# GpSimd sums that wait for the VectorE sum ahead of them in the list

## The chip, the cores and the metric

The kernel runs on one core of a Trainium2 chip. The metric is the device time of one execution in microseconds. The five engines of the core work in parallel, each through its own queue in order: TensorE (PE in the profile) multiplies matrices, VectorE (DVE) and ScalarE (ACT) do elementwise work and empty the matmul results, GpSimd (POOL) does elementwise work between tiles in SBUF and issues the loads, SyncE (SP) issues the stores. An engine waits for another by a semaphore.

## The reference

Eight batches of eight heads, 576 tokens, head dimension 64, 32 memory slots; then a bilinear feed-forward block over all 4608 tokens.

```python
def _attn_ref(q, k, v, phi):
    a = phi - np.max(phi, axis=2, keepdims=True)
    a = np.exp(a)
    a = a / (np.sum(a, axis=2, keepdims=True) + 1e-09)
    k_m = np.einsum('bhsm,bhsd->bhmd', a, k)
    v_m = np.einsum('bhsm,bhsd->bhmd', a, v)
    scores = scale * np.matmul(q, k_m.transpose(0, 1, 3, 2))
    ...
    attn = attn / (np.sum(attn, axis=-1, keepdims=True) + 1e-09)
    return np.matmul(attn, v_m)

def _moe_ref(x, w_a, w_b, w_out):      # x: 4608 x 512, w_a and w_b: 512 x 1536, w_out: 1536 x 512
    a = x @ w_a
    b = x @ w_b
    return a * b @ w_out
```

## The kernel before

**An order written out by hand.** The whole kernel is a list of some 1,500 short steps, the string `PLAN`. A loop at the end reads it from left to right and calls one function for each step; each function appends its instructions to the queues of its engines. So the list sets the order of the instructions on every engine, and two engines are tied to each other only by the data that they hand on. The steps of eight batches are interleaved, so that the attention of the later batches runs between the feed-forward matmuls of the earlier ones.

**The steps that matter here.** `a4.7.0` is one half of the product of attention and folded weights for batch 4, block 7 of 128 columns of the hidden layer, first half of the tokens: two matmuls into a PSUM bank `pa` (L724), copied by ScalarE to `a_sb` (L728). `b4.7.0` does the same for the other weight into `pb`, and VectorE multiplies `a_sb` by `pb` into `ht` (L731). One operand of that product lies in PSUM. `d3` takes three matmuls of the last matrix product (`two_downs`, L651), and now and then the sums that empty its banks. `6ed`, `6sm0`, `6tn0`, `6tn1`, `6ad` belong to the softmax over the slots of batch 6: a transposition, sums, normalisation on GpSimd and VectorE, a transposition back. `7exp0` is an exponential on ScalarE. `v7`, `p5`, `q3` and so on issue loads from GpSimd's queue.

**Seven products instead of eight.** From batch 5 on, many of the 2x2 block products of the hidden layer are done in seven matmul products instead of eight (function `seven`, steps such as `P5.4.6`), and so are the last ones (`two_downs`). This needs sums and differences of the operands beforehand, all of them between tiles in SBUF:

- `h8.2` and `g8.3`: sums of the hidden layer for the last product, 128x768 (`sum_tokens`, L635), four for each pair of blocks; `h` on GpSimd, `g` on VectorE.
- `5S11P`, `5S01D`: sums of the folded weights of batch 5, 128x512 (`v_sum`, L530); `P` on GpSimd, `D` on VectorE. The first digit behind S is which sum, the second which third of the columns. `P5.4.6` needs `5S11P`, `P5.4.5` needs `5S21P`.
- `5T1P`, `5T2D`: sums of the attention of batch 5, 128x288 (`a_sum`, L538), with the same letters.
- `T30` on GpSimd and `V31` on VectorE: sums of the last weights, 128x768 (`sum_weights`, L618).
- `H7.4` on GpSimd and `J5.4` on VectorE: the products that finish a block of `seven` (L778).

All of these, and the normalisations of L475 and L499, are `tensor_tensor` instructions with two operands in SBUF. Which engine takes a step is written in its name.

**PSUM.** Its eight banks are given out in turn by `Banks`; a tile that takes a bank waits until the last reader of the bank's former tile is done.

Of the kernel before, what the change touches and what calls it, by code (L numbers as in the profile page):

```python
# [11 lines left out]
ALU = mybir.AluOpType  # L12
# [32 lines left out]
a3.10.1 b3.10.1 a3.8.1 b3.11.0 a3.2.1 h5.3 d3 a3.5.1 d1 5tn0 b3.5.1 6qt0 d1 a3.7.1 a3.11.1 b3.7.1 d2 6exp0 4x0b1 d1  # L45
a4.0.0 b3.2.1 d4 a3.9.1 5sm1 h6.0 d1 b3.8.1 h6.1 d3 5tn1 d2 4v2b 4x2b0 4x2b1 4v1a 4x1a1 6kv 4v2a 4x2a0 d1 q7 6km1 d1
6km0 d3 a3.4.1 b3.4.1 4x1a0 d1 g6.2 b3.11.1 h7.3 d4 b3.9.1 6qt3 d4 a4.0.1 a4.2.1 d3 6kvt d5 h7.0 5ad 4x2a1 5T0P d4 6sc
6e0 5v1a d2 5x1a1 b4.0.1 b4.2.1 a4.3.0 d7 6e1 7qt0 5x1a0 a4.9.1 d1 b4.3.0 b4.0.0 a4.1.1 a4.6.0 7qt3 5v0a 5T2D 5x0a0
5v0b 5v1b 5x1b0 5x0a1 g7.1 g8.0 d1 5T1P 5T3P g7.2 5x1b1 b4.6.0 5S01D g8.1 d3 v7 5S11P 5S21P a4.7.0 5S31P d1 g8.3 d3
h8.2 d3 6ed d3 P5.4.1 d2 b4.7.0 d1 5x0b1 d3 a4.6.1 b4.6.1 5x0b0 5S00P d4 7exp0 6sm0 d3 a4.2.0 b4.2.0 d1 a4.9.0 P5.4.6  # L50
b4.1.1 a4.10.1 6tn0 d3 b4.9.0 P5.4.5 d1 P5.4.7 a4.1.0 b4.1.0 a4.8.0 b4.8.0 a4.4.1 d5 P5.4.2 P5.4.4 P5.5.1 P5.5.2
P5.4.3 d2 a4.4.0 b4.4.0 d2 7qt2 d2 P5.5.5 d2 b4.9.1 P5.5.6 a4.5.0 d3 P5.5.3 a4.11.0 b4.5.0 5v2a 5x2a0 5x2a1 5v2b
a4.10.0 6sm1 d1 5S10P b4.10.1 5x2b1 d1 5S30P 5x2b0 d2 P5.5.7 b4.4.1 a4.7.1 a4.3.1 5S20P d2 b4.10.0 d2 P5.5.4 b4.11.0
b4.7.1 J5.4 6tn1 P5.1.1 a4.11.1 a4.8.1 d3 P5.1.6 g9.0 h9.3 d1 P5.1.2 d2 h9.1 P5.2.1 H5.5 b4.8.1 P5.1.5 d5 P5.2.5 d1
P5.2.2 P5.1.7 a4.5.1 P5.2.6 P5.1.3 d4 P5.6.1 h9.2 d1 H5.1 P5.1.4 P5.2.3 P5.2.7 a5.11.0 P5.7.1 b4.3.1 H5.2 d4 P5.7.2
P5.6.5 P5.2.4 b4.11.1 d1 P5.7.6 b4.5.1 h10.0 d6 P5.6.6 P5.6.2 P5.7.5 P5.7.7 h10.3 P5.6.3 d2 P5.6.7 a5.10.1 P5.0.1 d4
b5.10.1 P5.7.4 7exp1 a5.8.0 P5.7.3 d3 H5.6 P5.0.5 d1 P5.6.4 6ad H5.7 P5.3.1 P5.0.6 6T0P d2 b5.8.0 d3 a5.8.1 P5.0.3
P5.0.2 P5.0.7 d5 P5.3.6 a5.10.0 d3 6T1P 6T3P P5.3.5 P5.0.4 P5.3.7 P5.3.2 d4 P5.3.3 H5.0 d3 P5.3.4 H5.3 6v0a 6x0a1 7kv
7km1 6x0a0 6v0b 6x0b0 6v2b 6x2b1 7km0 6T2P d2 6x2b0 d6 7qt1 d4 a5.11.1 b5.11.0 a5.9.0 b5.10.0 6x0b1 7kvt d1 b5.9.0 d5
h10.1 6v1a 6x1a0 7sc 7e0 6x1a1 d1 g10.2 6S00P 6S10D 6S20D d1 g11.0 d1 b5.11.1 7e1 d4 b5.8.1 d5 6v1b 6x1b0 6S01P 7v1a  # L60
g11.1 6v2a d1 6S30D 6x2a1 d5 a5.9.1 7x1a0 d3 7ed 7x1a1 d1 7sm0 d8 b5.9.1 6x1b1 P6.3.1 P6.1.1 d4 7sm1 6x2a0 P6.1.2
h11.2 P6.3.2 6S11P 6S31P d4 P6.3.5 d2 P6.3.6 d4 a6.11.0 P6.3.3 d1 P6.3.7 a6.10.1 b6.11.0 g11.3 d1 P6.1.5 H6.3 6S21D
a6.8.0 d2 P6.2.5 7tn1 d2 g12.0 a6.10.0 P6.2.1 P6.3.4 P6.1.6 d2 h12.1 d4 P6.2.2 P6.2.6 P6.2.3 P6.1.3 P6.1.7 d2 P6.0.1
d5 P6.0.5 d1 P6.2.7 d2 P6.6.1 H6.2 P6.0.6 d2 P6.1.4 d1 P6.2.4 H6.1 d4 h12.2 d1 P6.0.2 P6.6.6 d2 P6.0.7 b6.10.0 d2
P6.5.1 P6.6.5 d2 P6.0.4 P6.6.7 a6.9.0 P6.0.3 7tn0 H6.0 P6.5.6 d1 P6.6.2 d1 P6.6.3 H6.6 d5 P6.5.2 7ad 7T0P d1 P6.4.1
P6.5.5 P6.5.7 d3 P6.4.5 h12.3 P6.6.4 d6 P6.4.6 P6.4.2 P6.4.3 P6.5.4 P6.5.3 H6.5 d5 P6.7.5 d1 P6.4.7 P6.7.1 d5 7T1P
b6.8.0 P6.4.4 d2 P6.7.6 P6.7.3 7v0a 7x0a0 7v1b 7x1b1 P6.7.7 7x0a1 b6.9.0 d2 7x1b0 d2 P6.7.2 P6.7.4 d4 a6.8.1 d2 7T3D
7v2b 7x2b1 7S01D 7S11D 7v2a g13.0 7x2a1 J6.7 7x2a0 7v0b d1 a6.11.1 d4 g13.1 d10 7S21D d1 7x0b0 d2 7S31D g13.2 J6.4
7S00D h13.3 7x0b1 P7.4.1 7T2D d2 b6.10.1 d2 7x2b0 7S10P d2 P7.4.2 d5 P7.4.6 b6.11.1 d1 P7.4.5 P7.7.1 P7.7.2 a7.8.0 d2
P7.4.3 P7.5.1 a6.9.1 P7.4.7 P7.7.6 b6.8.1 b7.8.0 b6.9.1 7S30P H7.4 d1 P7.4.4 d1 P7.7.5 P7.7.7 d4 7S20P P7.5.2 a7.11.0  # L70
d1 a7.10.0 P7.5.6 d4 P7.7.3 P7.7.4 P7.6.1 b7.10.0 P7.5.5 a7.9.0 P7.5.7 J7.7 P7.6.6 d5 P7.1.1 d2 h14.0 g14.1 d1 P7.5.3
H7.5 P7.5.4 d2 P7.1.5 P7.6.2 h14.2 P7.6.5 P7.6.7 P7.1.6 d2 b7.11.0 d2 P7.0.1 P7.1.3 P7.1.7 P7.6.3 h14.3 P7.6.4 d6
P7.0.2 d8 H7.1 P7.1.2 b7.9.0 P7.2.1 P7.0.5 P7.0.6 P7.1.4 d4 P7.2.2 P7.3.1 d1 P7.2.5 P7.0.7 P7.0.3 d1 H7.0 d5 P7.2.6 d1
P7.0.4 H7.6 P7.3.6 d1 a7.10.1 P7.2.7 b7.10.1 P7.3.5 P7.3.7 a7.9.1 d3 P7.3.2 d3 P7.2.4 P7.3.4 a7.8.1 g15.0 g15.1 g15.2
# [6 lines left out]
def kernel(  # L81
# [11 lines left out]
    nc = tc.nc  # L93

    B, H, S, D = q.shape
# [6 lines left out]
    HALF = S // 2  # L102
# [70 lines left out]
    def load_w(x, lo, hi):  # L173
        nc.gpsimd.dma_start(out=w_sbs[x][:, :, lo:hi], in_=(wa_rows, wb_rows)[x][:, :, lo:hi])
# [6 lines left out]
    ht = consts.tile([P, NFF, 2 * S], F16, name="ht")  # L181
# [51 lines left out]
    nc.vector.memset(kv_sbs[0][:, 2], 1.0 / CS)  # L233
    for x in halves:
        nc.vector.tensor_copy(out=kvs[0][:, 0, x], in_=k_f32[:, x])
    def issue(x):

        b, _, half = x[1:].partition(".")
        if x[0] == "w":
            lo, hi = x[2:].split(":")  # L240
            load_w("ab".index(x[1]), int(lo), int(hi))
        elif x[0] == "o":
            load_wo(int(b))
        elif x[0] == "p":
# [19 lines left out]
    attn = {}  # L264
# [13 lines left out]
    def units(b):  # L278
# [4 lines left out]
        t = {}  # L283
# [181 lines left out]
        def normalise(g, hfs=slice(0, 2)):  # L465
            if b not in attn:
                attn[b] = mid.tile([P, 2, S], F16, name="A")
            sl = slice(tokens(b, hfs.start).start, tokens(b, hfs.stop - 1).stop)
            if ("R", 0) not in t:
                both = spare.tile([P, 3, 512], F16, name="vsum1").rearrange("p z n -> p (z n)")  # L470
                for x in range(2):
                    t["R", x] = both[:, S * x:S * (x + 1)]
            nc.scalar.activation(out=t["R", g][:, sl], in_=t["L", g][:, sl], func=AF.Exp, scale=-1.0)
            engine = nc.vector if b < 2 else nc.gpsimd
            engine.tensor_tensor(out=attn[b][:, g, sl], in0=t["E"][:, g, sl], in1=t["R", g][:, sl], op=ALU.mult)  # L475

        def pairs(x):
            return x.rearrange("p g s -> p (g s)").bitcast(F32)
# [43 lines left out]
        def v_sum(n, y, engine):  # L522
            if (b, n) not in vsums:
                vsums[b, n] = spare.tile([P, 3, 512], F16, name=f"vsum{n}")
            S1, S2, S4 = (vsums[b, n][:, z] for z in range(3))
            sl = slice(512 * n, 512 * (n + 1))
            (A11, A12), (S3, A22) = ([vabs[b][z][:, g, sl] for g in range(2)] for z in range(2))
            out, in0, in1, op = ((S3, A11, S3, ALU.subtract), (S2, A22, S3, ALU.subtract), (S1, S2, A11, ALU.add),
                                 (S4, A12, S2, ALU.subtract))[y]
            engine.tensor_tensor(out=out, in0=in0, in1=in1, op=op)  # L530

        def a_sum(y, engine):
            if b not in asums:
                asums[b] = mid.tile([P, 4, HALF], F16, name="asum")
            T1, T2, T3, T4 = (asums[b][:, z] for z in range(4))
            (B11, B12), (B21, B22) = ([attn[b][:, g, HALF * z:HALF * (z + 1)] for z in range(2)] for g in range(2))
            out, in0, in1 = ((T1, B12, B11), (T2, B22, T1), (T3, B22, B12), (T4, B21, T2))[y]
            engine.tensor_tensor(out=out, in0=in0, in1=in1, op=ALU.subtract)  # L538

        def take_fold(lo, hi, z, gs=range(2)):  # L540
            first, second = b == 0 and hi <= 512, b < 2
# [71 lines left out]
    def sum_weights(x, part, engine):  # L613
        t = [t1_sum] + [w_sums[:, y] for y in range(3)]
        out, in0, in1 = ((t[0], quarter(0, 1), quarter(0, 0)), (t[1], quarter(1, 1), t[0]),
                         (t[2], quarter(1, 1), quarter(0, 1)), (t[3], quarter(1, 0), t[1]))[x]
        sl = slice(KH // 2 * part, KH // 2 * (part + 1))
        engine.tensor_tensor(out=out[:, sl], in0=in0[:, sl], in1=in1[:, sl], op=ALU.subtract)  # L618

    def tokens_of(cidx, x):  # L620
        pair, c = divmod(cidx, NI)
# [4 lines left out]
    def sum_tokens(n, x, engine):  # L626

        cidx = 2 * n
        if cidx not in h_sums:
            h_sums[cidx] = spool.tile([P, 4, KH, P], F16, name="h_sums")  # L630
        t = [h_sums[cidx][:, y] for y in range(4)]
        (a11, a12), (a21, a22) = ([tokens_of(cidx + y, z) for z in range(2)] for y in range(2))
        out, in0, in1, op = ((t[0], a21, a22, ALU.add), (t[1], t[0], a11, ALU.subtract),
                             (t[2], a12, t[1], ALU.subtract), (t[3], a11, a21, ALU.subtract))[x]
        engine.tensor_tensor(out=out, in0=in0, in1=in1, op=op)  # L635

    def store(o_sb, cidx, cs=slice(0, d_model), engines=(nc.sync, nc.sync)):
        pair, c = divmod(cidx, NI)
# [96 lines left out]
    def seven(k, b, i):  # L735
# [6 lines left out]
        x = sevens.setdefault((b, i), {})  # L742
# [15 lines left out]
        t0 = S * (b % 2)  # L758
        if k == 1:
            copy("z1", product("y", A11, B11, True))  # L760
        elif k == 5:
            copy("z5", product("v", S1, T1, True))
        elif k == 6:
            copy("z2", product("y", S2, T2, False))
        elif k == 3:
            plus("ah", product("v", S4, B22, False), "z2")
            banks.free(x["v"][1])
        elif k == 7:
            plus("bh", product("y", S3, T3, False), "z5")
        elif k == 2:  # L770
            plus("al", product("x", A12, B21, True), "z1")
            banks.free(x["x"][1])
        elif k == 4:
            nc.vector.tensor_tensor(out=ht[:, i, t0:t0 + HALF], in0=x["al"], in1=product("y", A22, T4, False), op=ALU.mult)
            banks.free(x["y"][1])
        else:
            engine = (nc.gpsimd, nc.vector)[k - 8]
            engine.tensor_tensor(out=ht[:, i, t0 + HALF:t0 + S], in0=x["ah"], in1=x["bh"], op=ALU.mult)  # L778

    us = {b: units(b) for b in range(B)}  # L780

# [57 lines left out]
```

## Time and profile before

| what | value |
|---|---|
| median of three runs | 235.48 us (235.48 to 235.69) |
| the profiled execution | 236.3 us |
| its span, first to last instruction | 234.6 us |
| granted TensorE clock, mean | 0.997 |
| VectorE tensor_tensor h_sums, 128x768 | 18 + 11 + 11, mean 604, 600 and 569 ns |
| GpSimd tensor_tensor h_sums, 128x768 | 18 + 7 + 7, mean 1671, 1643 and 1640 ns |
| VectorE and GpSimd vsum, 128x512 | mean 420 and about 1200 ns |

Times are in microseconds unless marked ns. In the groups, a row gives line, engine, operation, result and operands, shape, count, busy time, mean duration, and the idle time before. In a timeline, a row gives start, duration, engine, line, operation, and in brackets the idle time ahead of it with what ended it. Instructions that follow each other without a wait on VectorE are shown to overlap by about 0.08 us. Matmuls are pipelined: one with 256 columns is shown with 0.27 us, but the next can start 0.11 us after it.

### The profile page before, as it was taken

How to read it: one execution, taken by the hardware profiler on the slowest of the kernel's cores; microseconds unless marked ns; L12 is line 12 of the kernel's file. 1: busy time of each engine (PE TensorE's matmuls, PEld its weight loads, DVE VectorE, ACT ScalarE, POOL GpSimd, SP SyncE). 2: the span in 40 equal slices, each digit the busy share in tenths (PEclk: the TensorE clock that was granted, in tenths of full speed). 3: DMA queues.
4: the chain of work that ended last, by engine and by line, in shares of the span. 5: the costliest groups of instructions: out<-in, count | busy, mean ns of one | idle time of the engine just before them, and what ended most of it. 6: DMA issues, size and time to landing. Idle time of an engine off the chain costs nothing.

```text
span 234.6 us, 7504 instructions
## 1 busy us (share of the span) xinstructions
PE 215.2 (92%) x2906; PEld 163.6 (70%) x2906; DVE 198.9 (85%) x514; ACT 170.1 (72%) x450; POOL 141.0 (60%) x142
## 2 busy tenths in 40 slices
PE   1189889998999999999999999999999999999993
PEld 0142537676778788876877777887787878888882
DVE  3534899999987866899897999998999999999962
ACT  2206689977799898788898978877897679766330
POOL 7927233704539668494849497599484981772201
PEclk9999999999999999999999999999999999999998
DMA  6999999999999999299745813021303213032164
GB/s 233 234 199 256 205 205 205 206 258 258 208 291 242 221 208 283 26 284 214 180 75 118 156 37 90 2 68 27 92 3 89 51 43 91 14 79 67 26 158 112
DMA packets 26259, 34.09 MB, mean 145 GB/s; under 512 B 2000, under 2 KB 20304, under 8 KB 26224
## 3 DMA queue, kind: packets, MB, share of 16 engines
q0 software_dynamic: 19760, 23.14, 53.6%
q1 hardware_dynamic: 5952, 9.70, 15.5%
q10 hardware_dynamic: 512, 0.79, 1.0%
q8 instruction: 22, 0.36, 0.6%
q14 instruction: 13, 0.11, 0.1%
HBM read 42.47 MB, written 9.44 MB: 221 GB/s over the span
## 4 chain that ended last, share of the span: by engine, by line
PE 79%; DMA 10%; DVE 6%; POOL 2%; issue 1%; DVEq 0%; POOLq 0%
PE py L651 20%; PE pb L724 14%; PE pa L724 13%; PE pv L651 9%; DMA wb_sb<-in_moe_w_b_dram 6%; PE pva L513 5%; PE py L747 5%; PE px L651 5%; DMA kv_sb<-in_v_dram 4%; PE pv L747 2%; PE pkv L320 2%; DVE ht L731 1%; PE px L747 1%; DVE w_sums L618 1%; PE pscore L409 1%
## 5 line engine op out<-in xcount | busy, mean ns | idle before, releaser
L731 DVE TENSOR_TENSOR ht<-a_sb,pb 128x288 f16<-128x288 f16 (+2 forms) x144 | 60.7, 444 | 9.9 <-PE pb L724 3.8
L724 PEld LDWEIGHTS <-vab 128*128 128x128 f16 x576 | 55.2, 98 | 18.0 <-issue 4.9
L728 ACT CAST a_sb<-pa 128x288 f16<-128x288 f32 (+2 forms) x144 | 56.0, 415 | 15.9 <-PE pa L724 8.7
L724 PE MATMUL pa<-A,vab 128*128 128x288 f16 (+2 forms) x288 | 55.7, 286 | 1.1 <-DVE ht L731 0.7
L724 PE MATMUL pb<-A,vab 128*128 128x288 f16 (+2 forms) x288 | 55.2, 286 | 1.0 <-DVE ht L731 0.9
L651 PEld LDWEIGHTS <-h_sums 128*128 128x128 f16 x432 | 41.5, 98 | 10.0 <-issue 2.9
L545 ACT CAST vab<-pva 128x512 f16<-128x512 f32 x82 | 45.6, 614 | 3.1 <-PE pva L513 2.9
L635 POOL TENSOR_TENSOR h_sums<-ht 128x768 f16<-128x768 f16 x18 | 30.0, 1671 | 20.4 <-DVE ht L731 20.1
L651 PEld LDWEIGHTS <-ht 128*128 128x128 f16 x324 | 31.3, 98 | 7.0 <-issue 1.6
L651 PE MATMUL py<-w_sums,h_sums 128*128 128x256 f16 x216 | 35.6, 273 | 0.0
L651 PE MATMUL pv<-wo_sb,h_sums 128*128 128x256 f16 x216 | 35.1, 273 | 0.0
L752 ACT COPY z<-py 128x288 f32<-128x288 f32 x48 | 19.2, 413 | 6.6 <-PE py L747 5.3
L778 POOL TENSOR_TENSOR ht<-ah,bh 128x288 f16<-128x288 f16 x20 | 14.4, 734 | 11.1 <-DVE ah L756 8.4
L651 PE MATMUL py<-wo_sb,ht 128*128 128x256 f16 x108 | 19.4, 273 | 0.0
L651 PE MATMUL px<-wo_sb,ht 128*128 128x256 f16 x108 | 18.1, 273 | 0.0
L651 PE MATMUL py<-w_sums,ht 128*128 128x256 f16 x108 | 17.6, 273 | 0.0
L422 ACT ACTIVATE E<-pscore 128x288 f16<-128x288 f32 x28 | 9.6, 422 | 10.4 <-PE pscore L409 10.2
L658 ACT ACTIVATE u<-py 128x256 f32<-128x256 f32 x36 | 14.7, 408 | 3.2 <-PE py L651 2.8
L288 ACT ACTIVATE exp_sb<-phi_sb 128x576 f16<-128x576 f32 x16 | 11.0, 699 | 5.2 <-DMA phi_sb<-in_phi_dram 5.2
L635 POOL TENSOR_TENSOR h_sums<-h_sums,ht 128x768 f16<-128x768 f16 x7 | 11.5, 1640 | 5.1 <-DVE h_sums L635 4.7
L297 DVE STREAM_TRANSPOSE qT<-q_sb 128x288 f32<-128x288 f32 x28 | 12.3, 459 | 2.6 <-DMA q_sb<-in_q_dram 2.6
L747 PE MATMUL py<-asum,vab 128*128 128x288 f16 x48 | 13.2, 286 | 0.0
(106 smaller groups left out, 392.7 us busy)
## 6 DMA issues: line engine op xcount, KB each, us to landing
out_dram<-o_sb SPq DMA_DIRECT2D x68, 128.0 KB, 2.6
phi_sb<-in_phi_dram POOLq DMA_DIRECT2D x8, 576.0 KB, 9.0
kv_sb<-in_v_dram POOLq DMA_DIRECT2D x8, 576.0 KB, 10.9
kv_sb<-in_k_dram POOLq DMA_DIRECT2D x7, 576.0 KB, 11.9
q_sb<-in_q_dram POOLq DMA_DIRECT2D x6, 576.0 KB, 9.1
wo_sb<-in_moe_w_out_dram POOLq DMA_DIRECT2D x6, 256.0 KB, 14.0
wa_sb<-in_moe_w_a_dram POOLq DMA_DIRECT2D x2, 512.0 KB, 14.2
wb_sb<-in_moe_w_b_dram POOLq DMA_DIRECT2D x2, 512.0 KB, 16.6
```

The source lines that it names most:

```text
L297: nc.vector.transpose(out=t["qT"][:, hp, :].bitcast(F32), in_=qs[b][:, hp, :].bitcast(F32))
L513: nc.tensor.matmul(t["pva", lo, z][g][0][32 * j:32 * j + 32, 0:hi - lo], t["kvT"][64 * r:64 * r + 64, 4 + g if side else 2, M * j:M * j + ...
L545: engine_copy(out=vabs[b][z][:, g, lo:hi], in_=pva[:, 0:hi - lo])
L635: engine.tensor_tensor(out=out, in0=in0, in1=in1, op=op)
L651: nc.tensor.matmul(po, lhs[:, i], rhs[:, i], start=first and i == 0, stop=i == KH - 1, skip_group_check=not first)
L658: nc.scalar.mul(out=x, in_=po, mul=scale)
L724: nc.tensor.matmul(ps, vabs[b][x][:, g, P * i:P * (i + 1)], attn[b][:, g, ts], start=(g == 0), stop=(g == 1))
L728: nc.scalar.copy(out=a_sbs[b, i, hf][:, :n], in_=ps)
L731: nc.vector.tensor_tensor(out=ht[:, i, t0:t0 + n], in0=a_sbs.pop((b, i, hf))[:, :n], in1=ps, op=ALU.mult)
L747: nc.tensor.matmul(x[bank][0], lhs, rhs, start=first, stop=True, skip_group_check=True)
L752: nc.scalar.copy(out=x[name], in_=po)
L778: engine.tensor_tensor(out=ht[:, i, t0 + HALF:t0 + S], in0=x["ah"], in1=x["bh"], op=ALU.mult)
```

## The change

A helper `tt` issues the `tensor_tensor` instructions of the sums above. It remembers the last one that went to VectorE. The first GpSimd sum that follows it in the list gets a dependency on it: GpSimd waits until that VectorE sum is done. The memory is then empty until the next VectorE sum, so a second GpSimd sum right behind has no new wait. Products with an operand in PSUM do not go through `tt`.

In the list, six GpSimd sums stand further ahead: `5T1P` and `5T3P` ahead of `5T2D`; `h9.3` ahead of `J5.4`; `6S00P` ahead of `g10.2`; `h13.3` ahead of `7T3D`; `h14.0` ahead of `J7.7`. The order among the GpSimd steps stays as it was, and so does the order among the steps of every other engine.

```diff
-... 7qt3 5v0a 5T2D 5x0a0
-5v0b 5v1b 5x1b0 5x0a1 g7.1 g8.0 d1 5T1P 5T3P g7.2 5x1b1 b4.6.0 5S01D g8.1 d3 v7 5S11P 5S21P a4.7.0 5S31P d1 g8.3 d3
+... 7qt3 5v0a 5T1P 5T3P
+5T2D 5x0a0 5v0b 5v1b 5x1b0 5x0a1 g7.1 g8.0 d1 g7.2 5x1b1 b4.6.0 5S01D g8.1 d3 v7 5S11P 5S21P a4.7.0 5S31P d1 g8.3 d3
 h8.2 d3 6ed d3 P5.4.1 d2 b4.7.0 d1 5x0b1 d3 a4.6.1 b4.6.1 5x0b0 5S00P d4 7exp0 6sm0 d3 a4.2.0 b4.2.0 d1 a4.9.0 P5.4.6
...
-b4.7.1 J5.4 6tn1 P5.1.1 a4.11.1 a4.8.1 d3 P5.1.6 g9.0 h9.3 d1 P5.1.2 d2 h9.1 ...
+b4.7.1 h9.3 J5.4 6tn1 P5.1.1 a4.11.1 a4.8.1 d3 P5.1.6 g9.0 d1 P5.1.2 d2 h9.1 ...
...
-h10.1 6v1a 6x1a0 7sc 7e0 6x1a1 d1 g10.2 6S00P 6S10D 6S20D d1 g11.0 ...
+h10.1 6v1a 6x1a0 7sc 7e0 6x1a1 d1 6S00P g10.2 6S10D 6S20D d1 g11.0 ...
...
-b6.8.0 ... d4 a6.8.1 d2 7T3D
-7v2b 7x2b1 7S01D 7S11D 7v2a g13.0 7x2a1 J6.7 7x2a0 7v0b d1 a6.11.1 d4 g13.1 d10 7S21D d1 7x0b0 d2 7S31D g13.2 J6.4
-7S00D h13.3 7x0b1 P7.4.1 7T2D d2 b6.10.1 d2 7x2b0 7S10P d2 P7.4.2 ...
+b6.8.0 ... d4 a6.8.1 d2 h13.3
+7T3D 7v2b 7x2b1 7S01D 7S11D 7v2a g13.0 7x2a1 J6.7 7x2a0 7v0b d1 a6.11.1 d4 g13.1 d10 7S21D d1 7x0b0 d2 7S31D g13.2
+J6.4 7S00D 7x0b1 P7.4.1 7T2D d2 b6.10.1 d2 7x2b0 7S10P d2 P7.4.2 ...
...
-... a7.9.0 P7.5.7 J7.7 P7.6.6 d5 P7.1.1 d2 h14.0 g14.1 d1 P7.5.3
+... a7.9.0 P7.5.7 h14.0 J7.7 P7.6.6 d5 P7.1.1 d2 g14.1 d1 P7.5.3
 H7.5 P7.5.4 d2 P7.1.5 ...
...
+    turn = {}
+
+    def tt(engine, **operands):
+
+        x = engine.tensor_tensor(**operands)
+        if engine is nc.vector:
+            turn["last"] = x
+        elif "last" in turn:
+            tc.add_manual_dep(x.ins, turn.pop("last").ins.name,
+                              mybir.DependencyInfo(mybir.DependencyClass.Sync, mybir.DependencyReason.DATA),
+                              reason="turns of the two engines")
+        return x
+
...
-            engine.tensor_tensor(out=out, in0=in0, in1=in1, op=op)
+            tt(engine, out=out, in0=in0, in1=in1, op=op)
```

The last two lines stand for seven places: the sums of L475, L499, L530, L538, L618, L635 and L778 call `tt` with the operands that they had.

More of the change, by code (lines that the diff above doesn't have):

```diff
@@ L47 @@
 6km0 d3 a3.4.1 b3.4.1 4x1a0 d1 g6.2 b3.11.1 h7.3 d4 b3.9.1 6qt3 d4 a4.0.1 a4.2.1 d3 6kvt d5 h7.0 5ad 4x2a1 5T0P d4 6sc
-6e0 5v1a d2 5x1a1 b4.0.1 b4.2.1 a4.3.0 d7 6e1 7qt0 5x1a0 a4.9.1 d1 b4.3.0 b4.0.0 a4.1.1 a4.6.0 7qt3 5v0a 5T2D 5x0a0
-5v0b 5v1b 5x1b0 5x0a1 g7.1 g8.0 d1 5T1P 5T3P g7.2 5x1b1 b4.6.0 5S01D g8.1 d3 v7 5S11P 5S21P a4.7.0 5S31P d1 g8.3 d3
+6e0 5v1a d2 5x1a1 b4.0.1 b4.2.1 a4.3.0 d7 6e1 7qt0 5x1a0 a4.9.1 d1 b4.3.0 b4.0.0 a4.1.1 a4.6.0 7qt3 5v0a 5T1P 5T3P
+5T2D 5x0a0 5v0b 5v1b 5x1b0 5x0a1 g7.1 g8.0 d1 g7.2 5x1b1 b4.6.0 5S01D g8.1 d3 v7 5S11P 5S21P a4.7.0 5S31P d1 g8.3 d3
 h8.2 d3 6ed d3 P5.4.1 d2 b4.7.0 d1 5x0b1 d3 a4.6.1 b4.6.1 5x0b0 5S00P d4 7exp0 6sm0 d3 a4.2.0 b4.2.0 d1 a4.9.0 P5.4.6
@@ L53 @@
 a4.10.0 6sm1 d1 5S10P b4.10.1 5x2b1 d1 5S30P 5x2b0 d2 P5.5.7 b4.4.1 a4.7.1 a4.3.1 5S20P d2 b4.10.0 d2 P5.5.4 b4.11.0
-b4.7.1 J5.4 6tn1 P5.1.1 a4.11.1 a4.8.1 d3 P5.1.6 g9.0 h9.3 d1 P5.1.2 d2 h9.1 P5.2.1 H5.5 b4.8.1 P5.1.5 d5 P5.2.5 d1
+b4.7.1 h9.3 J5.4 6tn1 P5.1.1 a4.11.1 a4.8.1 d3 P5.1.6 g9.0 d1 P5.1.2 d2 h9.1 P5.2.1 H5.5 b4.8.1 P5.1.5 d5 P5.2.5 d1
 P5.2.2 P5.1.7 a4.5.1 P5.2.6 P5.1.3 d4 P5.6.1 h9.2 d1 H5.1 P5.1.4 P5.2.3 P5.2.7 a5.11.0 P5.7.1 b4.3.1 H5.2 d4 P5.7.2
@@ L59 @@
 7km1 6x0a0 6v0b 6x0b0 6v2b 6x2b1 7km0 6T2P d2 6x2b0 d6 7qt1 d4 a5.11.1 b5.11.0 a5.9.0 b5.10.0 6x0b1 7kvt d1 b5.9.0 d5
-h10.1 6v1a 6x1a0 7sc 7e0 6x1a1 d1 g10.2 6S00P 6S10D 6S20D d1 g11.0 d1 b5.11.1 7e1 d4 b5.8.1 d5 6v1b 6x1b0 6S01P 7v1a
+h10.1 6v1a 6x1a0 7sc 7e0 6x1a1 d1 6S00P g10.2 6S10D 6S20D d1 g11.0 d1 b5.11.1 7e1 d4 b5.8.1 d5 6v1b 6x1b0 6S01P 7v1a
 g11.1 6v2a d1 6S30D 6x2a1 d5 a5.9.1 7x1a0 d3 7ed 7x1a1 d1 7sm0 d8 b5.9.1 6x1b1 P6.3.1 P6.1.1 d4 7sm1 6x2a0 P6.1.2
@@ L66 @@
 P6.5.5 P6.5.7 d3 P6.4.5 h12.3 P6.6.4 d6 P6.4.6 P6.4.2 P6.4.3 P6.5.4 P6.5.3 H6.5 d5 P6.7.5 d1 P6.4.7 P6.7.1 d5 7T1P
-b6.8.0 P6.4.4 d2 P6.7.6 P6.7.3 7v0a 7x0a0 7v1b 7x1b1 P6.7.7 7x0a1 b6.9.0 d2 7x1b0 d2 P6.7.2 P6.7.4 d4 a6.8.1 d2 7T3D
-7v2b 7x2b1 7S01D 7S11D 7v2a g13.0 7x2a1 J6.7 7x2a0 7v0b d1 a6.11.1 d4 g13.1 d10 7S21D d1 7x0b0 d2 7S31D g13.2 J6.4
-7S00D h13.3 7x0b1 P7.4.1 7T2D d2 b6.10.1 d2 7x2b0 7S10P d2 P7.4.2 d5 P7.4.6 b6.11.1 d1 P7.4.5 P7.7.1 P7.7.2 a7.8.0 d2
+b6.8.0 P6.4.4 d2 P6.7.6 P6.7.3 7v0a 7x0a0 7v1b 7x1b1 P6.7.7 7x0a1 b6.9.0 d2 7x1b0 d2 P6.7.2 P6.7.4 d4 a6.8.1 d2 h13.3
+7T3D 7v2b 7x2b1 7S01D 7S11D 7v2a g13.0 7x2a1 J6.7 7x2a0 7v0b d1 a6.11.1 d4 g13.1 d10 7S21D d1 7x0b0 d2 7S31D g13.2
+J6.4 7S00D 7x0b1 P7.4.1 7T2D d2 b6.10.1 d2 7x2b0 7S10P d2 P7.4.2 d5 P7.4.6 b6.11.1 d1 P7.4.5 P7.7.1 P7.7.2 a7.8.0 d2
 P7.4.3 P7.5.1 a6.9.1 P7.4.7 P7.7.6 b6.8.1 b7.8.0 b6.9.1 7S30P H7.4 d1 P7.4.4 d1 P7.7.5 P7.7.7 d4 7S20P P7.5.2 a7.11.0
-d1 a7.10.0 P7.5.6 d4 P7.7.3 P7.7.4 P7.6.1 b7.10.0 P7.5.5 a7.9.0 P7.5.7 J7.7 P7.6.6 d5 P7.1.1 d2 h14.0 g14.1 d1 P7.5.3
+d1 a7.10.0 P7.5.6 d4 P7.7.3 P7.7.4 P7.6.1 b7.10.0 P7.5.5 a7.9.0 P7.5.7 h14.0 J7.7 P7.6.6 d5 P7.1.1 d2 g14.1 d1 P7.5.3
 H7.5 P7.5.4 d2 P7.1.5 P7.6.2 h14.2 P7.6.5 P7.6.7 P7.1.6 d2 b7.11.0 d2 P7.0.1 P7.1.3 P7.1.7 P7.6.3 h14.3 P7.6.4 d6
@@ L474, in normalise @@
             engine = nc.vector if b < 2 else nc.gpsimd
-            engine.tensor_tensor(out=attn[b][:, g, sl], in0=t["E"][:, g, sl], in1=t["R", g][:, sl], op=ALU.mult)
+            tt(engine, out=attn[b][:, g, sl], in0=t["E"][:, g, sl], in1=t["R", g][:, sl], op=ALU.mult)
         def pairs(x):
@@ L498, in token_normalise @@
             engine = (nc.gpsimd, nc.vector)[x]
-            engine.tensor_tensor(out=v, in0=v, in1=sums.unsqueeze(2).to_broadcast(list(v.shape)), op=ALU.mult)
+            tt(engine, out=v, in0=v, in1=sums.unsqueeze(2).to_broadcast(list(v.shape)), op=ALU.mult)
         def a_turn():
@@ L537, in a_sum @@
             out, in0, in1 = ((T1, B12, B11), (T2, B22, T1), (T3, B22, B12), (T4, B21, T2))[y]
-            engine.tensor_tensor(out=out, in0=in0, in1=in1, op=ALU.subtract)
+            tt(engine, out=out, in0=in0, in1=in1, op=ALU.subtract)
         def take_fold(lo, hi, z, gs=range(2)):
@@ L617, in sum_weights @@
         sl = slice(KH // 2 * part, KH // 2 * (part + 1))
-        engine.tensor_tensor(out=out[:, sl], in0=in0[:, sl], in1=in1[:, sl], op=ALU.subtract)
+        tt(engine, out=out[:, sl], in0=in0[:, sl], in1=in1[:, sl], op=ALU.subtract)
     def tokens_of(cidx, x):
@@ L634, in sum_tokens @@
                              (t[2], a12, t[1], ALU.subtract), (t[3], a11, a21, ALU.subtract))[x]
-        engine.tensor_tensor(out=out, in0=in0, in1=in1, op=op)
+        tt(engine, out=out, in0=in0, in1=in1, op=op)
     def store(o_sb, cidx, cs=slice(0, d_model), engines=(nc.sync, nc.sync)):
@@ L777, in seven @@
             engine = (nc.gpsimd, nc.vector)[k - 8]
-            engine.tensor_tensor(out=ht[:, i, t0 + HALF:t0 + S], in0=x["ah"], in1=x["bh"], op=ALU.mult)
+            tt(engine, out=ht[:, i, t0 + HALF:t0 + S], in0=x["ah"], in1=x["bh"], op=ALU.mult)
     us = {b: units(b) for b in range(B)}
```

## The prediction

> **What bounds the kernel now.** I read the page first, then the waits of TensorE, then VectorE's groups by form, then the timelines around every place where the new rule could bite.
>
> ```profile
> span 234.6 us, 7504 instructions
> ...
> PE 215.2 (92%) x2906; PEld 163.6 (70%) x2906; DVE 198.9 (85%) x514; ACT 170.1 (72%) x450; POOL 141.0 (60%) x142
> ```
>
> TensorE is the bound and VectorE follows it closely; GpSimd has 40% to spare. So a change that only moves GpSimd's sums can help in one way: by letting VectorE answer TensorE sooner at a place where TensorE stands still for VectorE. The waits of TensorE over the whole span list few such places:
>
> ```profile
> PE pb L724 <- DVE ht L731: 0.9, 1, 0.9
> ...
> PE pa L724 <- DVE ht L731: 0.7, 1, 0.7
> ...
> PE py L747 <- DVE ht L774: 0.3, 1, 0.3
> ```
>
> Each is one single stall. VectorE's groups by form say where they come from. A VectorE sum of 128x768 takes 547 ns, but one of the same size took 1994:
>
> ```profile
> L618 DVE TENSOR_TENSOR w_sums<-wo_sb 128x768 f16<-128x768 f16 x4 | 2.1, 547 | 0.0
> L618 DVE TENSOR_TENSOR w_sums<-wo_sb,w_sums 128x768 f16<-128x768 f16 x1 | 2.0, 1994 | 0.0
> ```
>
> **The collision that I expect to go.** Here is the timeline of VectorE, of GpSimd and of TensorE at 132 to 137.5 us, one block for each: start, duration, engine, line, operation, in brackets the idle time before it and what ended it. The steps are, on VectorE, g8.1, g8.3, 6ed and two `ht` products; on GpSimd, 5S11P and 5S21P.
>
> ```profile
> 132.28 0.55 DVE L635 TENSOR_TENSOR h_sums<-h_sums,ht 128x768 f16<-128x768 f16 x1
> 132.75 1.51 DVE L635 TENSOR_TENSOR h_sums<-ht 128x768 f16<-128x768 f16 x1
> 134.18 0.77 DVE L482 STREAM_TRANSPOSE E<-E 128x576 f32<-128x576 f32 x1
> 134.87 0.78 DVE L731 TENSOR_TENSOR ht<-a_sb,pb 128x288 f16<-128x288 f16 x2
> ```
>
> ```profile
> 132.51 1.33 POOL L530 TENSOR_TENSOR vsum<-vab 128x512 f16<-128x512 f16 x1 [3.12 <-DVE vab L530]
> 133.93 1.35 POOL L530 TENSOR_TENSOR vsum<-vsum,vab 128x512 f16<-128x512 f16 x1
> ```
>
> ```profile
> 134.15 0.49 PE L651 MATMUL pv<-wo_sb,h_sums 128*128 128x256 f16 x3
> 135.34 0.41 PE L724 MATMUL pa<-A,vab 128*128 128x288 f16 x2 [0.70 <-DVE ht L731]
> ...
> 136.18 0.29 PE L747 MATMUL py<-asum,vsum 128*128 128x288 f16 x1
> ...
> 137.37 0.29 PE L747 MATMUL pv<-asum,vsum 128*128 128x288 f16 x1
> ```
>
> 5S11P starts at 132.51, while g8.1 runs, so it is queued when g8.1 ends at 132.28 + 0.55 = 132.83. g8.3, next on VectorE, then takes 1.51 instead of 0.55: it ends at 134.26, that is 0.42 after 5S11P's end at 133.84. The two sums ran one after the other. VectorE is 1.51 - 0.55 = 0.96 late, 6ed and the `ht` product follow without a gap, and the `pa` matmul, whose bank that product frees, waits. TensorE's last issue before it is at 134.15 + 2 x 0.11 = 134.37 (0.49 - 0.27 for two steps, with 0.27 for one matmul of 256), so its next slot is 134.48; it issues at 135.34. Lost: 0.70 by the row's modelled end, 0.86 by issue.
>
> **The change, part by part.** Only the first GpSimd sum behind a VectorE sum in the list gets the new wait; in the changed list these are 20 of the 84 GpSimd sums. For each I set the end of the VectorE sum against the start of the GpSimd sum. For 16 of them the VectorE sum had ended before; the smallest margins are h9.1 and its like, which need that very result already. A wait that is met costs nothing that I can place, and these I take at zero, with GpSimd's idle 40% as the cover. Four waits bind.
>
> (1) 5S11P waits for g8.1. What a GpSimd sum needs after a VectorE sum's end is shown by g9.0 and h9.1, which depend on each other today:
>
> ```profile
> 148.61 0.55 DVE L635 TENSOR_TENSOR h_sums<-ht 128x768 f16<-128x768 f16 x1
> ```
>
> ```profile
> 143.94 1.64 POOL L635 TENSOR_TENSOR h_sums<-ht 128x768 f16<-128x768 f16 x1 [0.16 <-DVE ht L731]
> 149.24 1.64 POOL L635 TENSOR_TENSOR h_sums<-h_sums,ht 128x768 f16<-128x768 f16 x1 [3.65 <-DVE h_sums L635]
> ```
>
> 149.24 - 149.16 = 0.08. So 5S11P starts at about 132.91, and g8.3 stands at VectorE since 132.75. Who goes first then is shown by g6.2 and h7.3, where the VectorE sum starts 0.17 before the GpSimd sum:
>
> ```profile
> 122.72 0.55 DVE L635 TENSOR_TENSOR h_sums<-ht,h_sums 128x768 f16<-128x768 f16 x1
> ...
> 122.89 1.88 POOL L635 TENSOR_TENSOR h_sums<-ht 128x768 f16<-128x768 f16 x1 [3.11 <-DVE ht L731]
> ```
>
> VectorE keeps its 0.55 and GpSimd pays (1.88 against 1.64, ending 1.50 after the VectorE sum). So g8.3 ends at 133.30, VectorE gains 0.96, the `pa` matmul is free at about 134.4, and TensorE goes on in its slot at 134.48: a gain of 0.86, with 0.70 as its lower end by the row.
>
> That rule of order is also the Trainium skill's: "SBUF — State Buffer", section "SBUF: two separate sides", says that VectorE instructions with two SBUF inputs and GpSimd share a port pair as an exclusive lock, and that whichever starts first has it for the whole instruction. The 1.51 and the 1.88 agree with it.
>
> What is queued behind the wait: 5S11P ends at 133.30 + 1.50 less the difference of plain times, 1.64 - 1.16 (the same form at 198.28, below), so 134.32 instead of 133.84; 5S21P ends about 135.6 instead of 135.28, and all up to h9.3 moves by the same 0.3. Behind h9.3 GpSimd idles 3.65 us (row at 149.24), which swallows it. Who waits for them: P5.4.6 (TensorE at 136.18, then about 135.35) needs 5S11P, 1.0 to spare; P5.4.5 (137.37, then 136.55) needs 5S21P, 0.9 to spare. Cost nothing; without that cover it would be 0.3 to 0.5.
>
> What is late next is ScalarE, whose timeline there is:
>
> ```profile
> 134.44 0.53 ACT L658 ACTIVATE u<-py 128x256 f32<-128x256 f32 x1
> 134.72 0.82 ACT L288 ACTIVATE exp_sb<-phi_sb 128x576 f16<-128x576 f32 x1
> 135.78 0.40 ACT L728 CAST a_sb<-pa 128x288 f16<-128x288 f32 x1 [0.25 <-PE pa L724]
> 136.38 0.40 ACT L728 CAST a_sb<-pa 128x288 f16<-128x288 f32 x1 [0.20 <-DVE sum L492]
> ```
>
> The `a_sb` at 135.78 would be wanted at 134.92, but the exponential runs to 135.54; by the overlap of neighbours (134.97 against 134.72) the cast can start at 135.3, some 0.4 late. The next one, wanted at 135.52, is nearly in time, since the idle 0.25 and 0.20 are used up. TensorE needs that bank again only four tiles later. I charge 0.05 of 0 to 0.15. Net gain of (1): 0.8, between 0.55 and 0.86.
>
> (2) T30 waits for V31, and V31's own collision stays, since h1.0 stands ahead of V31 in the list:
>
> ```profile
> 55.82 1.88 POOL L635 TENSOR_TENSOR h_sums<-ht 128x768 f16<-128x768 f16 x1 [8.35 <-DVE ht L731]
> 57.68 1.94 POOL L618 TENSOR_TENSOR w_sums<-wo_sb,w_sums 128x768 f16<-128x768 f16 x1
> ```
>
> ```profile
> 56.13 1.99 DVE L618 TENSOR_TENSOR w_sums<-wo_sb,w_sums 128x768 f16<-128x768 f16 x1
> ```
>
> ```profile
> 62.03 0.27 PE L651 MATMUL py<-w_sums,ht 128*128 128x256 f16 x1
> ```
>
> V31 runs from 56.13 to 58.12 (the 1994 ns), so the stall of 0.9 on `pb` remains. T30 would start at 58.20 and take its plain 1.64, ending at 59.84 instead of 59.62. Behind it on GpSimd's queue stand load issues, 0.2 later; nothing in the waits after 57 us is put down to a load. TensorE reads T30's tile at 62.03. Zero; by its nearest row, h7.3's 0.24, it could reach 0.2 if that slack were not there.
>
> (3) h7.3 waits for g6.2 (rows above): start 123.35, end about 124.95, 0.2 late. The 3.12 us of idle before 5S11P swallow it. Zero.
>
> (4) 7S10P waits for 7T2D:
>
> ```profile
> 198.28 1.16 POOL L530 TENSOR_TENSOR vsum<-vab 128x512 f16<-128x512 f16 x1 [5.08 <-DVE vab L530]
> ...
> 201.04 0.73 POOL L778 TENSOR_TENSOR ht<-ah,bh 128x288 f16<-128x288 f16 x1 [0.38 <-DVE bh L756]
> ```
>
> ```profile
> 198.03 0.30 DVE L538 TENSOR_TENSOR asum<-A 128x288 f16<-128x288 f16 x1
> ```
>
> 7T2D ends at 198.33; 0.08 to 0.2 late, inside the 0.38 of idle before H7.4. Zero.
>
> The six moves (5T1P, 5T3P, h9.3, 6S00P, h13.3, h14.0) pass VectorE, ScalarE and TensorE steps only, no GpSimd step and no load, so GpSimd's order is unchanged. They keep these six from a wait that would hurt. Against the kernel before they are worth zero.
>
> After 136 us TensorE waits only once more (the 0.3 on `py`), so 0.8 won at 134.5 should arrive at the end. The sum: 236.3 of the profiled execution (span 234.6 and 1.7 around it) - 0.8 = 235.5. The median of 235.48 is 0.82 below the profiled time; I carry the difference over: 234.7. The 5S11P collision hangs on instructions of VectorE alone (5S01D releases 5S11P, g8.1 follows it), so it should stand in every execution.
>
> **The rivals.** No gain: at g8.1's end g8.3 and the freed 5S11P race, and 5S11P is first again. For it: by the "whichever starts first" above, 0.1 would decide. Against: g8.3 stands ready since 132.75. Then nothing changes but 0 to 0.15 of later start: 235.5. The same time comes out if the runs without a profile don't have the collision.
>
> Half a gain: ScalarE's lateness reaches TensorE fully, 0.86 - 0.43 = 0.4: 235.1.
>
> Slower: GpSimd, held at 5S11P, stays late and blocks VectorE further on. The place is h9.3 in front of J5.4, VectorE's next sum. h9.3 ends at 145.58 now, 145.9 by my sum; J5.4 moves from its place just ahead of g9.0 (148.61) to about 147.0. If the hold is over 1.1 us longer than I have it, h9.3 keeps J5.4 waiting, up to its 1.64. By V31's rows, where 1.44 of VectorE became 0.92 of TensorE, and by g8.3's, where 0.96 became 0.86, that costs 1.0 to 1.5, net of the gain +0.2 to +0.7: up to 236.2. Nothing in the rows makes the hold that long.
>
> **How the numbers follow.** Forecast, 234.4 to 234.95: 0.69. No gain, 235.5: 0.12. Half, 235.1: 0.04. Slower, 235.7 to 236.2: 0.15. The range from 234.4 to 235.6 takes in the first three, 0.85. The bound of 0.2%, about what a measurement of this kernel can tell, is 0.47 us: faster 0.69, same 0.12 + 0.04 = 0.16, slower 0.15.
>
> **What would show it.** Right: g8.3 at about 0.55, 5S11P starting after g8.1's end and taking about 1.4, no idle before the `pa` matmul near 134.5; V31 still near 2 us; T30 and h7.3 at plain 1.64. Wrong: g8.3 still at 1.5 (no gain), ScalarE named as the releaser of a new TensorE wait near 135 (half), or a VectorE sum over 1 us after 140 that is short today (slower).

## The result and the profile after

| | kernel before | changed kernel |
|---|---|---|
| first comparison, median of 6 runs each | 235.58 us | 234.39 us |
| ratio, 95% interval | | 0.9946 (0.9931 to 0.9962) |
| second comparison, medians of 26 and 12 runs | 235.43 us | 234.60 us |
| ratio, 95% interval | | 0.9957 (0.9936 to 0.9977) |
| profiled execution: time, span | 236.3, 234.6 us | 234.21, 232.5 us |

Faster, as forecast, with 234.39 against 234.7 forecast; the range began at 234.4, so the time lies 0.01 us outside it. The page of the changed kernel, and the lines of its TensorE's waits for `pa`, `pb` and `py` on VectorE (waiting step, releaser, us in total, times, longest); the 0.5 is at 23 us:

```profile
span 232.5 us, 7507 instructions
...
PE 214.8 (92%) x2906; PEld 163.7 (70%) x2906; DVE 196.6 (85%) x514; ACT 169.9 (73%) x450; POOL 140.6 (60%) x142
```

```profile
PE pa L737 <- DVE A L240: 0.5, 1, 0.5
PE py L760 <- DVE ht L787: 0.3, 1, 0.3
```

All sums now carry line 240, that of the helper; other lines have moved down by 13. Two waits of the kernel before are gone: `pa` for `ht` (0.7), as forecast, and `pb` for `ht` (0.9), which was not. The 0.5 at 23 us is not new: it is 0.3 in the kernel before, for `A`. VectorE, GpSimd, TensorE and ScalarE of the changed kernel at the first place:

```profile
131.03 0.55 DVE L240 TENSOR_TENSOR h_sums<-h_sums,ht 128x768 f16<-128x768 f16 x1
131.50 0.55 DVE L240 TENSOR_TENSOR h_sums<-ht 128x768 f16<-128x768 f16 x1
131.96 0.77 DVE L495 STREAM_TRANSPOSE E<-E 128x576 f32<-128x576 f32 x1
```

```profile
131.72 1.33 POOL L240 TENSOR_TENSOR vsum<-vab 128x512 f16<-128x512 f16 x1 [3.29 <-ACT u L671]
133.14 1.15 POOL L240 TENSOR_TENSOR vsum<-vsum,vab 128x512 f16<-128x512 f16 x1
```

```profile
132.90 0.49 PE L664 MATMUL pv<-wo_sb,h_sums 128*128 128x256 f16 x3
133.23 0.41 PE L737 MATMUL pa<-A,vab 128*128 128x288 f16 x2
```

```profile
133.47 0.82 ACT L301 ACTIVATE exp_sb<-phi_sb 128x576 f16<-128x576 f32 x1
134.04 0.84 ACT L741 CAST a_sb<-pa 128x288 f16<-128x288 f32 x2
```

g8.1 ends at 131.58, 5S11P starts at 131.72, 0.14 later, and g8.3, which stands there since 131.50, takes 0.55. (The bracket of 5S11P names ScalarE; that the wait for g8.1 is what holds it is shown by the run below in which it is the only new wait, and whose bracket names VectorE's sum.) The `pa` matmul follows in its slot (132.90 + 3 x 0.11 = 133.23). Start against start, the `pv` matmuls in front of this place are 1.25 us earlier than in the profile before (134.15 against 132.90), the `pa` matmul 2.11 (135.34 against 133.23): 0.86 is won here, and from here to the end the 2.11 stays.

The 1.25 came at the second place, V31 and h1.0:

```profile
55.67 0.55 DVE L240 TENSOR_TENSOR h_sums<-ht,h_sums 128x768 f16<-128x768 f16 x1
56.14 0.55 DVE L240 TENSOR_TENSOR w_sums<-wo_sb,w_sums 128x768 f16<-128x768 f16 x1
```

```profile
55.84 2.35 POOL L240 TENSOR_TENSOR h_sums<-ht 128x768 f16<-128x768 f16 x1 [8.31 <-DVE ht L744]
58.16 1.63 POOL L240 TENSOR_TENSOR w_sums<-wo_sb,w_sums 128x768 f16<-128x768 f16 x1
```

The `pb` matmul no longer waits there. h1.0 starts where it did, 55.84 against 55.82, but now V31 (at 56.14) goes first, and h1.0 takes 2.35 instead of 1.88. The new wait there, T30's, lies behind both. Did it bring this, or chance?

### The profile page after: what moved, and what is told of

Read it like the earlier page. It is cut to its first block, busy times and chain, and to the rows that moved or that the text cites. A ratio compares the mean times of both kernels' runs of the same rounds, so it can differ in the third digit from the quotient of the medians.

```text
span 232.5 us, 7507 instructions
## 1 busy us (share of the span) xinstructions
PE 214.8 (92%) x2906; PEld 163.7 (70%) x2906; DVE 196.6 (85%) x514; ACT 169.9 (73%) x450; POOL 140.6 (60%) x142
## 4 chain that ended last, share of the span: by engine, by line
PE 83%; DMA 10%; DVE 2%; POOL 2%; issue 1%; POOLq 0%
PE py L664 21%; PE pb L737 15%; PE pa L737 14%; PE pv L664 10%; DMA wb_sb<-in_moe_w_b_dram 6%; PE pva L526 5%; PE px L664 5%; PE py L760 5%; DMA kv_sb<-in_v_dram 4%; PE pv L760 2%; PE pkv L333 2%; PE px L760 1%; PE pscore L422 1%; PE pD L475 1%; PE pk L387 1%
```

## The experiments

**The kernel before again** (no edit).

> The kernel before, unchanged, for the spread of its times and a second look at its trace. In the profiled execution on record V31 took 1.99 us and g8.3 1.51 us (0.55 each without a GpSimd sum), and TensorE stood for them 1.25 and 0.86 us. Theory A (which sum goes first is settled anew in each execution): the times fall into groups that lie 0.86 or 1.25 us apart, and this look may show another set of slow sums. A reading of A that fits the times known: 235.5 is V31 slow and g8.3 not, 236.3 is both. Theory B (the queues settle it): V31 at 2.0 and g8.3 at 1.5 again, and times near 236.3 in the profile and 0.8 lower without it.

Median 235.26 of 12 runs, from 235.01 to 236.81. VectorE at 56 us, then VectorE, GpSimd and TensorE at 131 to 134 us, in this second profile:

```profile
56.16 0.55 DVE L618 TENSOR_TENSOR w_sums<-wo_sb,w_sums 128x768 f16<-128x768 f16 x1
```

```profile
131.50 1.51 DVE L635 TENSOR_TENSOR h_sums<-ht 128x768 f16<-128x768 f16 x1
```

```profile
131.26 1.33 POOL L530 TENSOR_TENSOR vsum<-vab 128x512 f16<-128x512 f16 x1 [3.11 <-DVE vab L530]
```

```profile
134.09 0.41 PE L724 MATMUL pa<-A,vab 128*128 128x288 f16 x2 [0.70 <-DVE ht L731]
```

V31 takes 0.55 in the kernel before too. So the 1.99 of the first profile does not come in every execution, while g8.3's 1.51 and the 0.70 came again. The times form no clean groups. This profile is the one to set beside that of the changed kernel: g8.3 starts at 131.50 in both, the `pa` matmul behind it is 0.86 us apart (134.09 against 133.23), and the spans are 233.3 and 232.5 us. The whole difference between these two executions is made at this one place.

**T30's wait alone.**

```diff
-                tc.add_manual_dep(...)            # in each first GpSimd sum
+            if turn["step"] == "T30":
+                tc.add_manual_dep(...)            # list as before
```

> One wait alone: T30 waits for V31; list as before, no other new wait. Theory T (T30, queued without a wait behind h1.0, is what lets h1.0 go ahead of V31): V31 takes 0.55, the TensorE stall at 58 us is gone, 1.1 to 1.25 us faster than the kernel before: about 234.3; g8.3 as in the kernel before. My prediction's theory (T30's wait is worth nothing): V31 as in the kernel before, no change in time.

Ratio 1.001 (0.9994 to 1.0026), g8.3 at 1.51, V31 at 0.55 as in the kernel before. The theory that T30, queued behind h1.0, lets h1.0 go ahead falls: in the second profile of the kernel before T30 was queued without a wait too, and V31 took 0.55. T30's wait is worth nothing that this interval shows.

**5S11P's wait alone**, the same edit with `"5S11P"`.

> One wait alone: 5S11P waits for g8.1; list as before, no other new wait. My prediction's theory: g8.3 takes 0.55, the 0.86 us stall of TensorE near 135 us is gone, 0.8 faster: 234.7. Theory T with chance in g8.3: g8.3 is slow in few executions of the kernel before, so the median moves by under 0.3 us (235.2 to 235.6), and only the slowest executions go; V31 still takes 2.0.

Ratio 0.9969 (0.9953 to 0.9984), median 234.63. VectorE's g8.1 and g8.3, and GpSimd's 5S11P:

```profile
132.45 0.55 DVE L240 TENSOR_TENSOR h_sums<-h_sums,ht 128x768 f16<-128x768 f16 x1
132.91 0.55 DVE L240 TENSOR_TENSOR h_sums<-ht 128x768 f16<-128x768 f16 x1
```

```profile
133.15 1.33 POOL L240 TENSOR_TENSOR vsum<-vab 128x512 f16<-128x512 f16 x1 [3.99 <-DVE h_sums L240]
```

One wait of the twenty gives 0.3%, and g8.3 is the place. The rival reading, that g8.3 is slow in few executions, falls: it took 1.50 or 1.51 in each of the six traces, one for each run, of a kernel that leaves 5S11P whole and without its wait.

**Everything but T30's wait**, the condition turned to `!= "T30"`, list as changed.

> The whole change without one wait: T30 does not wait for V31. Theory T: V31 is back at 2.0 and TensorE's stall at 58 us too, 1.1 to 1.25 us slower than the changed kernel: about 235.5. My prediction's theory: as fast as the changed kernel, 234.4. Theory A: a mixture of both.

Ratio 0.9961 (0.9947 to 0.9974), median 234.51, V31 at 0.55. As fast as the whole change, within the intervals.

**The changed kernel again**, beside the three that follow.

> The changed kernel, unchanged, for the spread of its times beside the kernel before on one chip. The times of the kernel before have a floor near 235.0 (span 233.2) and a tail up to 236.8; 5S11P's wait alone gave 0.7 us. If the whole change is worth no more than that wait, the median is 0.7 to 0.95 us below the kernel before. If the other 19 waits bring something (theory T and its like), it is 1.2 below, as in the first comparison. V31 at 0.55 or at 2.0 by chance.

Ratio 0.9957 (0.9936 to 0.9977): 0.83 between the medians, what 5S11P's wait alone gave (0.81) within the spread. V31 at 0.55, g8.3 at 0.55.

**All waits, none of the six moves** (list as before).

> All waits, and the list of the kernel before: the six sums are not moved. Then 5T1P waits for g8.0, h9.3 for g9.0, 6S00P for g10.2, h13.3 for 7S00D, h14.0 for J7.7 (or g13.2 and 7T2D's like ahead of it). By the trace 6S00P would start 1.9 us later, with 6S10D on VectorE behind it, and h13.3 6.5 us later, past the matmul that needs it, with 7S10P, 7S20P, h14.0 and h14.2 behind. My reading: 1.5 to 4 us slower than the changed kernel, 236 to 238.5. The other theory (the moves are worth nothing): 234.4.

240.84: ratio 1.0231 (1.0202 to 1.0259), 6.2 us over the changed kernel, more than the 1.5 to 4 that I read. The two longest of seven new waits of TensorE, then of VectorE in the order of time, and GpSimd's h13.3:

```profile
PE pv L664 <- DVE ah L769: 1.3, 1, 1.3
...
PE pv L760 <- DVE ah L769: 1.0, 1, 1.0
```

```profile
151.81 0.46 DVE L769 TENSOR_TENSOR ah<-pv,z 128x288 f16<-128x288 f32 x1 [1.33 <-POOL ht L240]
...
168.73 0.42 DVE L240 TENSOR_TENSOR vsum<-vab 128x512 f16<-128x512 f16 x1 [1.33 <-POOL vab L240]
...
209.75 0.56 DVE L240 TENSOR_TENSOR h_sums<-h_sums,ht 128x768 f16<-128x768 f16 x1 [1.75 <-POOL h_sums L240]
```

```profile
200.12 1.64 POOL L240 TENSOR_TENSOR h_sums<-ht 128x768 f16<-128x768 f16 x1 [6.96 <-DVE vab L240]
```

6S00P, held for g10.2, keeps VectorE's 6S10D waiting for 1.33 us, and h14.0, held for J7.7, keeps g14.1 waiting for 1.75, with `ah` and a matmul behind it. An `ah` at 151.81 waits 1.33 for a GpSimd product, behind h9.3. h13.3 itself is held for 6.96. The late GpSimd sums also meet other VectorE sums: one takes 1.08 at 131.26 and one 1.53 at 170.73, instead of 0.55. I had followed the held sums to the matmuls that read them and seen one of the three VectorE steps that need GpSimd.

**H6.3 behind 7tn1** (the changed kernel, one step moved). The helper ties a GpSimd sum only to the VectorE sum ahead of it in the list. H6.3 stands ahead of 6S21D there, so in the changed kernel it waits for g11.3 and is free to start while 6S21D runs.

```diff
-P6.1.5 H6.3 6S21D a6.8.0 d2 P6.2.5 7tn1 d2 g12.0
+P6.1.5 6S21D a6.8.0 d2 P6.2.5 7tn1 H6.3 d2 g12.0
```

> The changed kernel with H6.3 set behind 7tn1 in the list, so that it waits for 7tn1. Today H6.3 starts while 6S21D runs, goes ahead of 7tn1, and 7tn1 takes 1.22 instead of 0.68; TensorE then issues a py matmul 0.41 us late. If the mechanism of g8.3 holds here too: 7tn1 at 0.68, that gap gone, 0.4 us faster than the changed kernel, about 234.0. If g12.0 behind 7tn1 then collides with H6.3 instead: g12.0 at over 0.7 and no gain.

Median 234.33 against 234.60 of the changed kernel beside it. The ratios to the kernel before, 0.9947 (0.9927 to 0.9968) and 0.9957 (0.9936 to 0.9977), overlap, so the times alone don't show a gain; the medians of the spans, 232.2 of 9 runs and 232.75 of 12, lie 0.55 apart. 7tn1 on VectorE and H6.3 on GpSimd, in the changed kernel:

```profile
175.47 1.22 DVE L240 TENSOR_TENSOR E<-E,sum 128x512 f16<-128x512 f16 x1
```

```profile
175.36 0.78 POOL L240 TENSOR_TENSOR ht<-ah,bh 128x288 f16<-128x288 f16 x1 [1.56 <-DVE h_sums L240]
```

and with H6.3 moved:

```profile
176.12 0.68 DVE L240 TENSOR_TENSOR E<-E,sum 128x512 f16<-128x512 f16 x1
```

```profile
176.95 0.91 POOL L240 TENSOR_TENSOR ht<-ah,bh 128x288 f16<-128x288 f16 x1 [2.49 <-PE pv L664]
```

The same mechanism at another place: 7tn1 is at its plain 0.68, and TensorE's wait of 0.3 on `py` has left its list of waits.

**h1.0 behind V31** (the kernel before, one step moved and one wait).

```diff
-h1.0 g0.2 V31
+g0.2 V31 h1.0        # h1.0 waits for V31; no other new wait
```

> The kernel before with one wait: h1.0 stands behind V31 in the list and waits for it; nothing else. Theory A (h1.0 or V31 goes first by chance, and that makes the tail of the times of the kernel before): V31 at 0.55 in every execution, the median as in the kernel before within 0.2 us, and no times over about 235.9 other than those where the first loads came late; g8.3 stays at 1.5. If V31 is slow in most executions: 1 us faster.

Ratio 1.001 (0.9988 to 1.0032), 234.91 to 236.72. No change, and the tail of the times is still there. With this wait h1.0 can't go first, so h1.0 and V31 don't make that tail.

**5S11P in two halves** (the kernel before, no wait).

```diff
+            if (b, n, y) == (5, 1, 1):
+                for half in (slice(0, 256), slice(256, 512)):
+                    engine.tensor_tensor(out=out[:, half], in0=in0[:, half], in1=in1[:, half], op=op)
```

> The kernel before with 5S11P done in two halves of 256 columns, two GpSimd instructions behind each other; no new wait. Theory E (the two sums take turns, a whole instruction at a time): g8.3 gets its turn after the first half, takes about 0.95 instead of 1.51, and TensorE's stall near 135 us shrinks by 0.5: 234.9. Theory S (the two engines share, so that VectorE is late by the GpSimd work that lies beside it): the same work lies beside it, g8.3 stays near 1.5, no change.

VectorE, GpSimd and TensorE there:

```profile
132.10 1.02 DVE L639 TENSOR_TENSOR h_sums<-ht 128x768 f16<-128x768 f16 x1
```

```profile
131.86 1.79 POOL L532 TENSOR_TENSOR vsum<-vab 128x256 f16<-128x256 f16 x2 [3.11 <-DVE vab L534]
```

```profile
134.21 0.40 PE L728 MATMUL pa<-A,vab 128*128 128x288 f16 x2 [0.21 <-DVE ht L735]
```

g8.3 is late by 0.47 instead of 0.96, and TensorE waits 0.21 instead of 0.70. The same GpSimd work in two instructions holds VectorE for half as long: here the two engines take turns by the instruction. The time moved by 0.9984 (0.9965 to 1.0003), which alone would not show it.

**Two waits and one move** (the list of before with H6.3 behind 7tn1; 5S11P waits for g8.1, H6.3 for 7tn1, nothing else).

> The list of the kernel before, with H6.3 alone moved (behind 7tn1), and two waits alone: 5S11P for g8.1, H6.3 for 7tn1. If these two collisions are all that can be won here and the other waits and moves cancel, it is as fast as the changed kernel with H6.3 moved: 0.45% to 0.55% below the kernel before, about 234.2; g8.3 at 0.55 and 7tn1 at 0.68. If the other waits or moves bring something of their own, it is slower than that kernel by it.

Median 234.01, ratio 0.9942 (0.9919 to 0.9965), g8.3 at 0.55 and 7tn1 at 0.68. It beats the kernel before. The two changed kernels were not run beside it; its spans (median 232.15 of 6 runs) lie 0.6 below the changed kernel's (232.75 of 12) and beside those of the changed kernel with H6.3 moved (232.2 of 9). So the other 18 waits, and the six moves that keep sums clear of them, bring nothing that shows.

**Two more profiles of the kernel before.**

> The kernel before again, one look. Theory A (chance) for V31: in the first execution it took 1.99 us, in eight other looks at kernels that leave h1.0 and V31 as they are 0.55; so 0.55 is likelier here. g8.3 at 1.51, as in each look so far at a kernel without 5S11P's wait.

> As the look before it: V31 at 0.55 more likely than 2.0, g8.3 at 1.51 in any case.

V31 0.55 both times, g8.3 1.51 and 1.50. In thirteen traces with h1.0 ahead of V31 in the list, V31 was slow in one: the one that I predicted from.

## Why the prediction was right or wrong

**The collision at g8.3: right, in place, cause and size.** 5S11P's wait alone brings 0.3% and takes g8.3 from 1.51 to 0.55. "Who goes first then" is as read from g6.2 and h7.3: with the wait, 5S11P starts 0.22 us after g8.3 does (131.72 against 131.50), and VectorE keeps its 0.55. The "no gain" rival, that 5S11P would be first again, fell in each of the seven traces of a kernel with the wait. The Trainium skill's rule ("SBUF — State Buffer", section "SBUF: two separate sides"), an exclusive lock for the whole instruction, agrees with the split sum: 0.47 instead of 0.96. That whichever starts first has it does not fit every place by the starts that the profile shows: h1.0 starts 0.3 us ahead of V31 and mostly goes second (last section).

**ScalarE's term in (1): charged 0.05, measured zero.** The first cast to `a_sb` is late about as I worked it out: it starts at 134.04, inside the exponential's record (133.47 to 134.29), 0.81 behind the `pa` matmul's start where it was 0.44 before. But no wait of TensorE comes of it, and TensorE keeps the full 0.86.

**"T30: zero", "h7.3: zero", "7S10P: zero", the other sixteen waits: right together, as far as the intervals tell.** The change without T30's wait, the whole change and 5S11P's wait alone gave 0.9961, 0.9957 and 0.9969, with intervals that overlap. **The moves** are worth what I said only in kind: without them the waits cost 6 us.

**The step that failed: the size of "Net gain of (1): 0.8, between 0.55 and 0.86", and the low end of 234.4 that was set by it.** 235.48 less 0.86 is 234.62; that left 0.2 for the spread of the runs, about what the three runs that I had showed (235.48 to 235.69). In the first comparison the gain came out as 1.19 (0.9 to 1.6 by the interval) instead of 0.8. The runs show in its place 0.86 by the traces and 0.83 (0.5 to 1.5) by the second comparison, whose median, 234.60, lies inside the range. The spread was put too small: 74 executions of the kernel before go from 234.87 to 237.46 with a median of 235.49, and of the 18 of the changed kernel in the two comparisons (234.19 to 235.42) eight lie under 234.4. So a median of six could fall on either side of 234.4, and that this one fell 0.01 below it is in part luck. Whether the rest of the 1.19 is more than chance stays open: no trace shows a second place in the changed kernel that is faster than in the second profile of the kernel before. One part of the spread is at the start: in the profile of 5S11P's wait alone V31 begins at 57.16 instead of 56.16, a microsecond late before the changed step.

**"The stall of 0.9 on `pb` remains": wrong, and by luck without effect on the number.** V31 takes 0.55 in the changed kernel, but so it does in the three later traces of the kernel before, so the change did not bring it. I took the profiled execution as the usual one, longer by 0.82 in any case, and carried the 0.82 over. Later profiled executions of the same kernel took 235.01, 235.36 and 235.25 us, no longer than others; the first held V31's rare stall, 1.25 us by the time it reached g8.3. The subtraction took it out unseen, and the base of 235.48 that it left agrees with the 235.49 of the 74 executions.

**"Slower", h9.3 in front of J5.4:** didn't happen; the one sum after 140 us that is slow in the changed kernel (7tn1) was slow before.

## What to carry to other kernels

When two engines' elementwise instructions take turns, look for a VectorE instruction that is longer than its kind and ask whether TensorE stands behind it: of the five in the first trace two, g8.3 and 7tn1, held TensorE in every trace of the kernel before, and one wait each removed them, for 7tn1 with its GpSimd sum moved. The rule of the changed kernel removes only g8.3's. Two more, near 73 and 78 us (1.09 and 0.74), stay slow in it, but no wait of TensorE lies there, and they cost nothing that shows. A blanket rule needs its exceptions moved out of the way (6 us here without them), so place the waits singly. And profile a second execution of the kernel before predicting from the first: one stall of 1.25 us was in one trace of thirteen.

## What the runs showed of the hardware that was not expected

A GpSimd sum that starts ahead of the next VectorE sum, by the profile, does not always go first. h1.0 starts 0.3 us ahead of V31, during g0.2, and V31 still goes first in twelve of thirteen traces, with h1.0 taking 2.35 us; 5S11P starts 0.24 us ahead of g8.3, during g8.1 (131.26 against 131.50 in the second profile), and goes first in all six traces that leave it whole and without its wait, as H6.3 does against 7tn1 from 0.1 us ahead (175.36 against 175.47 in the changed kernel). What decides was not found; nothing was tried that shifts one start by a tenth of a microsecond.
